# Separate PSUM tiles for the first feed-forward, W2 group 0 converted straight into SBUF, and eight float32 head pairs

## The chip, the cores and the metric

The kernel runs on one core of one Trainium2 chip. The metric is the device time of one execution in microseconds, lower is better. Engines are named as in the profile: PE is TensorE, DVE VectorE, ACT ScalarE, POOL GpSimd and SP the engine that issues the transfers.

## The reference

Three stages in a row: attention in which all scores lower than the row's maximum by more than tau are dropped, a feed-forward with SoLU and a layer norm, and a second, wider feed-forward with Mish.

```python
def _attn_ref(q, k, v, tau):                 # batch 4, heads 8, seq 576, head_dim 64
    scores = scale * np.matmul(q, k.transpose(0, 1, 3, 2))
    thresh = np.max(scores, axis=-1, keepdims=True) - tau
    scores = np.where(scores >= thresh, scores, -1000000000.0)
    scores = scores - np.max(scores, axis=-1, keepdims=True)
    attn = np.exp(scores)
    attn = attn / (np.sum(attn, axis=-1, keepdims=True) + 1e-09)
    return np.matmul(attn, v).astype(np.float32)

def _moe_ref(x, w_in, w_out, g_ln):          # 2304 tokens, 512 -> 1024 -> 512
    h = x @ w_in
    e = np.exp(h - np.max(h, axis=-1, keepdims=True))
    solu = h * (e / (np.sum(e, axis=-1, keepdims=True) + 1e-09))
    mu = np.mean(solu, axis=-1, keepdims=True)
    var = np.mean((solu - mu) ** 2, axis=-1, keepdims=True)
    ln = (solu - mu) / np.sqrt(var + 1e-06) * g_ln
    return (ln @ w_out).astype(np.float32)

def _moe2_ref(x, w_in, w_out):               # 512 -> 2048 -> 512
    h = x @ w_in
    sp = np.where(h > 20.0, h, np.log1p(np.exp(np.minimum(h, 20.0))))
    return ((h * np.tanh(sp)) @ w_out).astype(np.float32)
```

## The kernel before

**Numbers in two halves.** Most products are made from operands split into a high half in float32r and a low half (the difference), so that one float32 product becomes three float32r products (high by high, low by high, high by low). The four weight matrices come as float64 and are converted on the chip in blocks of 128 by 256: ACT makes a part from the low words (line 402) and clears the sign of the high words (line 408), DVE clamps and shifts (lines 410, 411) and joins the bits (line 413), POOL adds the two parts (line 415). `cr`, `cz`, `cl` and `cf` have two buffers each. Then ACT copies the high half and POOL subtracts for the low half.

**The order is planned.** Every step is a task with an engine, an estimated duration (`act`, `dve`, `gps`, `pe`, `dma`), what it waits for, and the buffers that it takes and uses. `Plan.run` tries several list schedules against these estimates and emits the instructions of each engine in the order of the shortest one. The engines then run in that order, and semaphores hold an instruction until its operands are there. Which instruction waits for which is worked out from the tiles that they read and write.

**Attention** goes over 16 pairs of heads; each pair has four blocks of 128 queries for each head and one block that the two heads share. `s_tile` makes scores on PE (line 505) in a PSUM buffer of two banks, DVE takes the maximum (line 511), ACT the exponential (line 513), DVE the threshold (line 516), POOL scales by the row's sum (line 530), PE transposes (lines 551, 554). For pairs from `F0` on, the transposed weights leave PSUM as a high half (ACT, line 538) and a low half (DVE, line 539), V is split too (lines 472, 473), and the products with V are two float32r products (line 588); the two halves of the result are added on POOL (line 605). Pairs before `F0` keep float32: one copy (line 536) and one float32 product (line 586).

**First feed-forward.** For each tile of 128 tokens `moe_h` makes h (line 642) in two halves of 512 columns, each taken out by ACT (line 650); `layer_norm` follows; `moe_t` transposes the result through the same PSUM buffer (line 692, taken out by lines 697 and 699); `moe_y` makes 256 tokens' y (line 713), taken out by ACT and DVE as high and low half (lines 723, 724) and stored. In PSUM all of this lies in one tile of two banks:

```python
    ms = pools(c1, PSUM)("p_ms").tile([128, 2, 512], F32, name="ms")
    smt = ms[:, 1, :PN]
    ...
    b_mo, b_s3 = Fixed(ms[:, 0]), Fixed(ms)
```

h and the transposes use the first bank (`b_mo`), y the second (`smt`), and in the first `M0` = 4 pairs a third of the score blocks uses both (`b_s3`).

**Second feed-forward.** W2 (both matrices of the second feed-forward) is used in four groups of 512 hidden features. `split_w2` brings a group into SBUF as AH, AL (first matrix) and BH, BL (second). Groups from `LATE` on are converted straight into these tiles: the conversion then clears the sign on DVE (line 405) and not on ACT, and the two halves are written by lines 825 (ACT) and 827 (POOL). Groups before `LATE`, here group 0, are converted ahead, stored to DRAM (line 428), loaded again (line 840) and split there (lines 847, 851). Group 0's tiles exist from `o_a` on, that is when the last scores and transposes of attention are done; those of group 1 from `o_c` on, when the first feed-forward is done. `ff_in` makes h (line 882), Mish and its two halves; `ff_out` makes o (line 908). The first `U0` = 6 pieces of group 0 are 256 tokens wide and run between the last tiles of the first feed-forward.

Of the kernel before, what the change touches and what calls it, by code (L numbers as in the profile page):

```python
# [8 lines left out]
F32 = mybir.dt.float32  # L9
# [3 lines left out]
ALU = mybir.AluOpType  # L13
# [9 lines left out]
class Task:  # L23
    def __init__(self, eng, dur, fn):
        self.eng, self.dur, self.fn = eng, dur, fn
# [13 lines left out]
class Buf:  # L39
# [4 lines left out]
    def new(self):  # L44
        self.slots.append(Slot(self, len(self.slots)))
        return self.slots[-1]


class Fixed(Buf):


    def __init__(self, part):
        super().__init__(None, None, None, None)
        self.part = part

    def new(self):
        x = super().new()
        x.take = lambda: setattr(x, "tile", self.part)
        return x


class Plan:
# [15 lines left out]
    def add(self, eng, dur, fn, deps=(), new=(), use=(), order=(), port=False, table=None):  # L78

        t = Task(eng, dur, fn)
        t.port, t.table = port or eng == "POOL", table
        t.new = list(new)
        t.need = [(d, True) for d in deps if d is not None] + [(d, False) for d in order if d is not None]
        for x in t.new:
            x.taker = t
            x.users.append(t)  # L90
        for x in use:
            x.users.append(t)
        self.tasks.append(t)
        return t
# [146 lines left out]
def kernel(  # L241
# [30 lines left out]
    PN = 256  # L272
    NG = 4
    FG = KF2 // NG
    NP = NT // PN
    F0 = 7
    M0 = 4
    LATE = 1
    U0 = 6

    def f(ap):
        return ap.bitcast(F32)

    def pools(stack, space=None, side=None):
        def pool(name, bufs=1):
            kw = {"space": space} if space is not None else {}
            if side is not None:
                kw["side"] = side
            return stack.enter_context(tc.tile_pool(name=name, bufs=bufs, **kw))
        return pool  # L290

    def act(n, psum=False):
        return (0.05 if psum else 0.094) + n / 1200

    def dve(n):
        return 0.069 + n * 1.042e-3
# [2 lines left out]
        return 0.069 + n * 0.52e-3  # L299

    def gps(n):
        return 0.149 + n * 2.1e-3

    def pe(count, n, passes=1):
        return count * (n / 2270 + 0.007 if passes == 1 else n * passes / 2400)
# [15 lines left out]
    def buf(p, tag, shape, dtype=F32, bufs=1):  # L321
        return Buf(lambda: P[p], tag, shape, dtype, bufs)
# [5 lines left out]
    wts = pool("wts")  # L328
    P["mo"] = pool("mo")
    P["small"] = small = pool("small")  # L330
    ms = pools(c1, PSUM)("p_ms").tile([128, 2, 512], F32, name="ms")
    smt = ms[:, 1, :PN]

    ident = const.tile([128, 128], F32, name="ident")
    tau_c = const.tile([128, 1], F32, name="tau_c")
# [118 lines left out]
    b_xo, b_tm = (buf("xs", n, [128, S], F32, c) for n, c in (("xo", 1), ("tm", 1)))  # L454
    b_st = buf("p_st", "st", [128, 2, 512], F32, 2)
    b_ta = buf("p_ta", "ta", [128, 512], F32, 2)
    b_mo, b_s3 = Fixed(ms[:, 0]), Fixed(ms)
    b_m = buf("small", "m", [128, 3], F32, 4)
    b_sr = buf("small", "sr", [128, 2], F32, 3)
    OPS, VL, E, EX, EVT, XST = ({} for _ in range(6))  # L460
    EXS, S3 = [], []

    def load_v(p):

# [11 lines left out]
    def operands(n):  # L476
        k2, q2, ks, qh, ql = (b.new() for b in (b_k2, b_q2, b_K, b_Q, b_L))
        lk, lq = (add("SP", dma(128 * w * 4), lambda slot=slot, src=src: D(slot.tile, src[n // H_, n % H_]), new=[slot])
                  for slot, src, w in ((k2, kk, S), (q2, qq, SP)))
        eng, e, cost = (V, "DVE", dve) if n < 2 else (G, "POOL", gps)  # L480
        a = add("ACT", act(S), lambda: SC.activation(ks.tile, k2.tile, ACTF.Copy), [lk], [ks], [k2])
        a2 = add(e, cost(S), lambda: eng.tensor_tensor(ks.tile[64:128], k2.tile[64:128], f(ks.tile[64:128]), ALU.subtract), [a], use=[ks, k2], port=True)  # L482
        b = add("ACT", act(SP), lambda: SC.activation(qh.tile, q2.tile, ACTF.Copy), [lq], [qh], [q2])  # L483
        b2 = add(e, cost(SP), lambda: eng.tensor_tensor(ql.tile, q2.tile, f(qh.tile), ALU.subtract), [b], [ql], [qh, q2], port=True)  # L484
        OPS[n] = [a, a2, b, b2], ks, qh, ql
# [36 lines left out]
    def weigh(p, i):  # L522

        e, sr, _, *ts = E[p, i]
        r = lambda h: sr.tile[:, h:h + 1]
        w = [add("DVE", 0.07, lambda h=h: V.tensor_scalar(r(h), r(h), 1.0e-9, None, ALU.add), [t], use=[sr]) for h, t in enumerate(ts)]
        t = add("DVE", 0.08, lambda: V.reciprocal(sr.tile[:, :len(ts)], sr.tile[:, :len(ts)]), w, use=[sr])  # L527
        for h in range(len(ts)):
            x = lambda h=h: e.tile[:, h * S:(h + 1) * S]
            E[p, i].append(add("POOL", 0.17 + S / 1000, lambda x=x, h=h: G.tensor_scalar(x(), x(), zero, r(h), ALU.add, ALU.mult), [t], use=[e, sr]))  # L530

    def leave(x, n, dst, src, dep, tp):

# [99 lines left out]
    def moe_h(t, j):  # L633
        if j == 0:
            x_split(t)
            SO[t] = [b_so.new()]
        so, (xh, xl) = SO[t][0], XSL[t]
        h, last_t = b_mo.new(), None

        def go(kt):  # L640
            for x, (l, r) in enumerate(((xh, W1H), (xh, W1L), (xl, W1H))):
                TE.matmul(h.tile, l.tile[:, kt], r[:, kt, j * 512:(j + 1) * 512],  # L642
                          start=(kt == 0 and x == 0), stop=(kt == KD - 1 and x == 2))

        for kt in range(KD):
            last_t = add("PE", pe(3, 512), lambda kt=kt: go(kt), XSP[t] + [W1T[kt, c] for c in range(j * 512, j * 512 + 512, CW)],
                         [h] if kt == 0 else (), [h, xh, xl], order=[last_t])
            if t == j == kt == 0:
                last_t.need += [(x, True) for x in S3[-1:]]
        SO[t].append(add("ACT", act(512, True), lambda: SC.activation(so.tile[:, j], h.tile, ACTF.Copy), [last_t],  # L650
                         [so] if j == 0 else (), [so, h], order=SO[t][1:]))
        if j:
            layer_norm(t)
# [50 lines left out]
    def moe_y(p, j):  # L704
        lh, ll = LN[p]
        c, half = divmod(j, 2)
        cs = slice(c * 128, (c + 1) * 128)
        y = smt
        ks = range(half * KF // 2, (half + 1) * KF // 2)

        def go(k):
            for x, (l, r) in enumerate(((W2H, lh), (W2L, lh), (W2H, ll))):
                TE.matmul(y, l[:, k, cs], r.tile[:, k], start=(k == 0 and x == 0), stop=(k == KF - 1 and x == 2))  # L713

        deps = TEV[p] + [W2T[k, c * 128 // CW * CW] for k in ks]
        t = Y0.get((p, c))
        for k in ks:
            t = add("PE", pe(3, PN), lambda k=k: go(k), deps + ([t] if t else Y0.get("last", [])), use=[lh, ll])
        Y0[p, c] = t
        if half == 0:  # L720
            return
        yh, yl = (b.new() for b in b_yy)
        a = add("ACT", act(PN, True), lambda: SC.activation(yh.tile, y, ACTF.Copy), [t], [yh])  # L723
        b = add("DVE", dve(PN), lambda: V.tensor_tensor(yl.tile, y, f(yh.tile), ALU.subtract), [a], [yl], [yh])  # L724
        Y0["last"] = [a, b]
        YST.setdefault(p, []).append(add("SP", dma(PN * 512), lambda: D(y_hi[p][cs, :], f(yh.tile)), [a], use=[yh]))
        YST[p].append(add("SP", dma(PN * 512), lambda: D(y_lo[p][cs, :], f(yl.tile)), [b], use=[yl]))


    for p in range(NH // 2 + 1):  # L730
        if p < NH // 2:
            operands(2 * p)
            operands(2 * p + 1)
            load_v(p)
        for i in range(QT):
            if p < NH // 2:
                for h in range(2 if i < KT else 1):
                    s_tile(p, i, h)
                weigh(p, i)
                for h in range(2 if i < KT else 1):  # L740
                    turn(p, i, h)
                turn(p, i, 2)
            if p and i == 0:
                pv(p - 1, 0, 1)
                pv(p - 1, 1, 1)
            if p < NH // 2 and i == 2:
                pv(p, 0, 0)
                pv(p, 1, 0)
    end_c3 = [t for ts in EXS for t in ts]
    pieces = []  # L750
    for t in range(NTILE + 1):
# [8 lines left out]

    W, W2Q = {}, {}

    def opens(fn, deps):

        return add("-", 0.0, fn, deps)

    def open_a():
        c3.close()
        P["w2a"] = pools(ctx, side="right")("w2a")
# [1 line left out]
    def open_b():  # L771
        c2.close()
        pool = pools(ctx, side="right")
        P["ffa"] = pool("ffa")
        P["hoa"] = pools(ctx, PSUM, "right")("hoa")

    def open_c():
        c1.close()
        pool = pools(ctx)
        P["w2b"] = pool("w2b")  # L780
        P["ffb"] = pool("ffb")
        P["hob"] = pools(ctx, PSUM)("hob")
        oa = pool("oa")
        acc.append(oa.tile([128, KD, NT], F32, name="acc"))

# [212 lines left out]
```

## Time and profile before

| what | before |
|---|---|
| median of three runs (range), us | 998.83 (997.68 to 999.58) |
| the profiled execution, us | 997.51 |
| its span, first to last instruction, us | 995.7 |
| PE busy, us (share of the span) | 934.4 (94%) |
| DVE busy, us | 639.2 (64%) |
| ACT busy, us | 594.8 (60%) |
| POOL busy, us | 422.8 (42%) |
| granted TensorE clock | 1.0 in every slice |

A row of the profile gives start and length of instructions, or sums over groups of them; times count from the start of the span. Idle time in front of an instruction is put down to what released it. Matmuls overlap one another, and their ends are modelled, so what PE loses in a wait is read from the starts.

### The profile page before, as it was taken

How to read it: one execution, taken by the hardware profiler on the slowest of the kernel's cores; microseconds unless marked ns; L12 is line 12 of the kernel's file. 1: busy time of each engine (PE TensorE's matmuls, PEld its weight loads, DVE VectorE, ACT ScalarE, POOL GpSimd, SP SyncE). 2: the span in 40 equal slices, each digit the busy share in tenths (PEclk: the TensorE clock that was granted, in tenths of full speed). 3: DMA queues.
4: the chain of work that ended last, by engine and by line, in shares of the span. 5: the costliest groups of instructions: out<-in, count | busy, mean ns of one | idle time of the engine just before them, and what ended most of it. 6: DMA issues, size and time to landing. Idle time of an engine off the chain costs nothing. (4 is left out here: it accounts for less than half of the span.)

```text
span 995.7 us, 16654 instructions
## 1 busy us (share of the span) xinstructions
PE 934.4 (94%) x5648; PEld 813.3 (82%) x5648; DVE 639.2 (64%) x1827; ACT 594.8 (60%) x1205; POOL 422.8 (42%) x446
## 2 busy tenths in 40 slices
PE   4899999989899999999889999999999999999998
PEld 4777777779788988888779888988888888888887
DVE  6898999998889989899865223135555445322222
ACT  5888988988778788786767364245433343222210
POOL 2878777877565566555451110123433133100000
PEclk9999999999999999999999999999999999999999
DMA  4444433324342223322474222397555245403312
GB/s 139 120 123 133 123 116 120 99 88 139 98 143 71 94 70 97 123 73 72 126 252 138 71 68 96 112 359 259 166 175 188 74 158 159 143 5 108 125 54 74
DMA packets 99942, 123.32 MB, mean 124 GB/s; under 512 B 9105, under 2 KB 72209, under 8 KB 99857
## 3 DMA queue, kind: packets, MB, share of 16 engines
q1 hardware_dynamic: 99712, 122.26, 38.9%
q8 instruction: 45, 0.74, 0.3%
q14 instruction: 41, 0.33, 0.1%
q10 hardware_dynamic: 144, 0.00, 0.0%
HBM read 98.11 MB, written 24.12 MB: 123 GB/s over the span
## 5 line engine op out<-in xcount | busy, mean ns | idle before, releaser
L530 POOL TENSOR_SCALAR e<-e,zero,sr 128x576 f32<-128x576 f32 x144 | 122.6, 859 | 66.6 <-DVE sr L527 46.1
L415 POOL TENSOR_TENSOR cf<-cf,cl 128x256 uint32<-128x256 uint32 x96 | 72.7, 765 | 153.9 <-DVE cf L413 116.4
L513 ACT ACTIVATE e<-st,m,sc 128x576 f32<-128x576 f32 x132 | 109.8, 835 | 31.0 <-DVE m L512 23.5
L516 DVE SCALAR_TENSOR_TENSOR e<-st,m,e 128x576 f32<-128x576 f32 x132 | 107.0, 813 | 12.8 <-ACT e L513 11.2
L505 PE MATMUL st<-Kst,Qhh 128*128 128x288 f32 (+2 forms) x312 | 94.4, 323 | 16.5 <-DVE Kst L482 10.4
L511 DVE TENSOR_REDUCE m<-st 128x1 f32<-128x576 f32 x132 | 98.7, 750 | 10.1 <-PE st L505 9.4
L713 PE MATMUL ms<-LH,W2H 128*128 128x256 f32 x288 | 86.1, 299 | 11.2 <-ACT so L650 7.8
L551 PE MATMUL ta<-ident,e 128*128 128x128 f32 x576 | 85.3, 277 | 8.2 <-ACT eyh L536 2.2
L505 PE MATMUL st<-Kst,Qb 128*128 128x288 f32 (+2 forms) x312 | 84.8, 296 | 0.0
L551 PEld LDWEIGHTS ta<-ident,e 128*128 128x128 f32 x576 | 66.8, 141 | 20.3 <-POOL e L530 7.3
L713 PE MATMUL ms<-LL,W2H 128*128 128x256 f32 x288 | 81.2, 282 | 0.0
L713 PE MATMUL ms<-LH,W2L 128*128 128x256 f32 x288 | 81.2, 282 | 0.0
L505 PEld LDWEIGHTS st<-Kst,Qhh 128*128 128x128 f32 x312 | 60.4, 194 | 23.4 <-DVE Kst L482 10.8
L642 PE MATMUL ms<-W1H,XH 128*128 128x512 f32 x144 | 62.0, 431 | 11.2 <-DVE yl L724 6.2
L932 DVE TENSOR_TENSOR acc<-acc,o 128x512 f32<-128x512 f32 x36 | 24.8, 688 | 70.8 <-PE o L908 70.6
L713 PEld LDWEIGHTS ms<-LH,W2H 128*128 128x128 f32 x288 | 54.5, 189 | 16.7 <-ACT so L650 11.3
L505 PEld LDWEIGHTS st<-Kst,Qb 128*128 128x128 f32 x312 | 60.5, 194 | 1.0
L484 POOL TENSOR_TENSOR Qb<-Q,Qhh 128x640 fp32r<-128x640 f32 x30 | 47.7, 1589 | 28.9 <-ACT Qhh L483 24.0
L402 ACT ACTIVATE cl<-cr 128x256 uint32<-128x256 uint32 x96 | 41.2, 438 | 30.1 <-DMA cr<-w_in 18.6
L642 PE MATMUL ms<-W1H,XL 128*128 128x512 f32 x144 | 56.7, 394 | 0.0
L642 PE MATMUL ms<-W1L,XH 128*128 128x512 f32 x144 | 56.6, 393 | 0.0
L887 ACT ACTIVATE n<-h 128x512 f32<-128x512 f32 x36 | 21.5, 597 | 58.3 <-PE h L882 58.2
(186 smaller groups left out, 2963.5 us busy)
## 6 DMA issues: line engine op xcount, KB each, us to landing
y5h<-y_hi SPq DMA_DIRECT2D x26, 512.0 KB, 5.9
y5l<-y_lo SPq DMA_DIRECT2D x26, 512.0 KB, 6.8
cr<-w_in SPq DMA_DIRECT2D x48, 256.0 KB, 3.2
cr<-w_out SPq DMA_DIRECT2D x48, 256.0 KB, 2.9
Q<-qq SPq DMA_DIRECT2D x32, 320.0 KB, 3.0
K<-kk SPq DMA_DIRECT2D x32, 288.0 KB, 2.9
y2h<-y_hi SPq DMA_DIRECT2D x10, 512.0 KB, 4.4
y2l<-y_lo SPq DMA_DIRECT2D x10, 512.0 KB, 5.4
```

The costliest lines, as they stand in the source:

```text
L402: t2 = add("ACT", act(CW), lambda: SC.activation(cl.tile, cr.tile[:, :, 0], ACTF.Copy, scale=2.0 ** -29), [t_f], [cl], [cr])
L415: t = add("POOL", gps(CW), lambda: G.tensor_tensor(cf.tile, cf.tile, cl.tile, ALU.add), [t4, t2], use=[cl, cf])
L484: b2 = add(e, cost(SP), lambda: eng.tensor_tensor(ql.tile, q2.tile, f(qh.tile), ALU.subtract), [b], [ql], [qh, q2], port=True)
L505: TE.matmul(st.tile[:, j, c - j * HS:c - j * HS + w], q.tile[:, i * 128:(i + 1) * 128], ks.tile[:, k0:k0 + w], start=(y == x == 0), stop=( ...
L511: t = add("DVE", dve(S), lambda: V.tensor_reduce(m.tile[:, 2:3], x(), AX.XY, ALU.max, negate=True), [t], [m], [st])
L513: a = add("ACT", act(S, True) + 0.18, lambda: SC.activation(et(), x(), ACTF.Exp, bias=m.tile[:, 0:1], scale=sc), [t], [e] if h == 0 else ( ...
L516: t = add("DVE", dve(S) + 0.06, lambda: V.scalar_tensor_tensor(et(), x(), m.tile[:, 1:2], et(), ALU.is_ge, ALU.mult, accum_out=sr.tile[:, ...
L530: E[p, i].append(add("POOL", 0.17 + S / 1000, lambda x=x, h=h: G.tensor_scalar(x(), x(), zero, r(h), ALU.add, ALU.mult), [t], use=[e, sr]))
L551: TE.transpose(tp.tile[:, k * 128:(k + 1) * 128], e.tile[:, o:o + 128], ident)
L642: TE.matmul(h.tile, l.tile[:, kt], r[:, kt, j * 512:(j + 1) * 512], start=(kt == 0 and x == 0), stop=(kt == KD - 1 and x == 2))
L713: TE.matmul(y, l[:, k, cs], r.tile[:, k], start=(k == 0 and x == 0), stop=(k == KF - 1 and x == 2))
L932: d = add("DVE", dve(512), lambda sums=sums, o=o: V.tensor_tensor(sums(), sums(), wide(o), ALU.add), pes + old, use=[o])
```

## The change

The tile `ms` goes. In its place the third score buffer `s3` (two banks) has a pool of its own, which is closed when the last score block that uses it is done (`o_s`); two pools of one bank each are then opened, `p_mo` for h and the transposes, `p_sm` for y. y's tile is taken anew for each block of 128 output rows, and the plan orders its use as it does for all other buffers, instead of by the entry `Y0["last"]`. The class `Fixed` is no longer needed. The PSUM pools of the second feed-forward change sides (left and right of PSUM).

`LATE` goes from 1 to 0: group 0 of W2 is converted straight into its tiles like the others; nothing is stored ahead.

`F0` goes from 7 to 8: pair 7 has float32 products with V too.

The planner's estimates for POOL change: `gps`, the low half of K (0.1 us more), and the scaling at line 530 (0.8 instead of 0.17 + 576/1000).

```diff
-class Fixed(Buf):
-
-
-    def __init__(self, part):
-        super().__init__(None, None, None, None)
-        self.part = part
-
-    def new(self):
-        x = super().new()
-        x.take = lambda: setattr(x, "tile", self.part)
-        return x
...
-    F0 = 7
+    F0 = 8
     M0 = 4
-    LATE = 1
+    LATE = 0
     U0 = 6
...
     def gps(n):
-        return 0.149 + n * 2.1e-3
+        return 0.16 + n * 2.15e-3
...
-    ms = pools(c1, PSUM)("p_ms").tile([128, 2, 512], F32, name="ms")
-    smt = ms[:, 1, :PN]
+    c0 = ctx.enter_context(ExitStack())
+    P["p_s3"] = pools(c0, PSUM, "right")("p_s3")
...
-    b_mo, b_s3 = Fixed(ms[:, 0]), Fixed(ms)
+    b_mo, b_s3 = buf("p_mo", "mo", [128, 512]), buf("p_s3", "s3", [128, 2, 512])
+    b_sm = buf("p_sm", "sm", [128, PN])
...
+    def open_s():
+        c0.close()
+        for n in ("p_mo", "p_sm"):
+            P[n] = pools(c1, PSUM, "right")(n)
...
-        a2 = add(e, cost(S), lambda: eng.tensor_tensor(ks.tile[64:128], k2.tile[64:128], f(ks.tile[64:128]), ALU.subtract), [a], use=[ks, k2], port=True)
+        a2 = add(e, cost(S) + (0.1 if e == "POOL" else 0.0), lambda: eng.tensor_tensor(ks.tile[64:128], k2.tile[64:128], f(ks.tile[64:128]), ALU.subtract), [a], use=[ks, k2], port=True)
...
-            E[p, i].append(add("POOL", 0.17 + S / 1000, lambda x=x, h=h: G.tensor_scalar(x(), x(), zero, r(h), ALU.add, ALU.mult), [t], use=[e, sr]))
+            E[p, i].append(add("POOL", 0.8, lambda x=x, h=h: G.tensor_scalar(x(), x(), zero, r(h), ALU.add, ALU.mult), [t], use=[e, sr]))
...
-                last_t.need += [(x, True) for x in S3[-1:]]
+                last_t.need.append((o_s, True))
...
-        y = smt
+        if half == 0:
+            Y0[p, c, "y"] = b_sm.new()
+        y = Y0[p, c, "y"]
...
-            t = add("PE", pe(3, PN), lambda k=k: go(k), deps + ([t] if t else Y0.get("last", [])), use=[lh, ll])
+            t = add("PE", pe(3, PN), lambda k=k: go(k), deps + ([t] if t else []), [] if t else [y], [lh, ll, y])
...
-        Y0["last"] = [a, b]
...
+    o_s = opens(open_s, S3)
...
-        P["hoa"] = pools(ctx, PSUM, "right")("hoa")
+        P["hoa"] = pools(ctx, PSUM)("hoa")
...
-        P["hob"] = pools(ctx, PSUM)("hob")
+        P["hob"] = pools(ctx, PSUM, "right")("hob")
```

## Rows read from the trace of the kernel before

**Rows 1.** Busy us (and instructions) of each engine in three stretches.

```profile
core 0: us, PE busy (x) PEld busy (x) DVE busy (x) ACT busy (x) POOL busy (x), PEclk, DMA share, GB/s
250.00:490.00 240.00, 223.75 (x1555) 201.55 (x1555) 218.19 (x668) 189.53 (x386) 139.83 (x128) 1.00 0.30 91
490.00:650.00 160.00, 148.81 (x1097) 139.38 (x1097) 62.31 (x143) 84.10 (x165) 31.31 (x33) 1.00 0.42 134
650.00:996.00 346.00, 341.85 (x1697) 288.01 (x1696) 132.81 (x292) 110.55 (x220) 66.91 (x88) 1.00 0.44 144
```

**Rows 2.** PE's waits from 250 to 490 us: waiter, releaser; us, times, longest.

```profile
PE ms L642 <- DVE yl L724: 3.4, 5, 1.4
...
PE ms L713 <- ACT so L650: 3.0, 6, 0.7
...
PE ms L642 <- ACT yh L723: 2.5, 4, 1.5
```

**Rows 3.** PE's waits from 490 to 650 us.

```profile
PE ms L713 <- ACT so L650: 3.5, 5, 0.7
PE ms L642 <- DVE yl L724: 2.9, 3, 1.0
PE ms L713 <- DVE yl L724: 2.3, 2, 1.2
```

**Rows 4.** PE in order of time near 558 us: start, length, idle before, releaser.

```profile
557.37 0.40 PE L642 MATMUL ms<-W1L,XH 128*128 128x512 f32 x1
557.60 0.39 PE L642 MATMUL ms<-W1H,XL 128*128 128x512 f32 x1
558.97 0.50 PE L642 MATMUL ms<-W1H,XH 128*128 128x512 f32 x1 [0.98 <-DVE yl L724]
```

**Rows 5.** The chain that ended last: start us, length, what.

```profile
510.40 0.61 ACT so L650
...
511.67 1.48 PE h L882 x12
...
530.58 1.43 PE o L908 x12
```

**Rows 6.** PE in order of time, float32 products, then split products.

```profile
192.72 2.32 PE L586 MATMUL ta<-eyh,V 128*128 128x320 f32 x8
194.88 0.70 PE L586 MATMUL ta<-evh,V 128*128 128x320 f32 x2
...
492.27 0.31 PE L588 MATMUL ta<-eyh,V 128*128 128x320 f32 x1
...
493.60 0.31 PE L588 MATMUL ta<-eyl,V 128*128 128x320 f32 x1
```

**Rows 7.** Groups by line: busy us, mean ns | idle before.

```profile
L415 POOL TENSOR_TENSOR cf<-cf,cl 128x256 uint32<-128x256 uint32 x96 | 72.7, 765 | 153.9 <-DVE cf L413 116.4 <-ACT cl L402 19.3 <-issue 9.2
...
L413 DVE SCALAR_TENSOR_TENSOR cf<-cr,cz 128x256 uint32<-128x256 uint32 x96 | 45.8, 492 | 4.3 <-POOL AL L827 1.2 <-issue 0.5 <-DMA w2o<-cf 0.4
...
L410 DVE TENSOR_SCALAR cz<-cz 128x256 f32<-128x256 f32 x96 | 33.3, 359 | 1.8 <-ACT cz L408 1.1
...
L539 DVE TENSOR_TENSOR eyl<-ta,eyh 128x512 fp32r<-128x512 f32 x45 | 30.3, 684 | 1.5 <-ACT eyh L538 1.3
```

**Rows 8.** POOL in order of time, low halves of W2 group 1.

```profile
641.54 1.44 POOL L827 TENSOR_TENSOR AL<-cf,AH 128x256 fp32r<-128x256 f32 x2 [26.64 <-ACT AH L825]
...
676.09 0.74 POOL L827 TENSOR_TENSOR AL<-cf,AH 128x256 fp32r<-128x256 f32 x1 [0.53 <-ACT AH L825]
```

**Rows 9.** Instructions of W2 group 0's store and load: ns min/median/max, first and last start.

```profile
L428 SPq DMA_DIRECT2D w2i<-cf x8: 320/338/447, 267.5 to 467.6; - x8
...
L840 SPq DMA_DIRECT2D AL<-w2i x4: 395/428/891, 491.1 to 492.5; - x4
```

**Rows 10.** POOL and DVE in order of time near 509 us.

```profile
508.08 1.23 POOL L673 TENSOR_SCALAR so<-so,nmu,rs 128x1024 f32<-128x1024 f32 x1 [0.69 <-DVE rs L672]
...
508.56 0.91 DVE L410 TENSOR_SCALAR cz<-cz 128x256 f32<-128x256 f32 x1 [0.32 <-ACT cz L408]
```

More of the change, by code (lines that the diff above doesn't have):

```diff
@@ L461, with opens @@
     EXS, S3 = [], []
+    def opens(fn, deps):
+        return add("-", 0.0, fn, deps)
+    def open_s():
+        c0.close()
+        for n in ("p_mo", "p_sm"):
+            P[n] = pools(c1, PSUM, "right")(n)
     def load_v(p):
@@ L712, in go @@
             for x, (l, r) in enumerate(((W2H, lh), (W2L, lh), (W2H, ll))):
-                TE.matmul(y, l[:, k, cs], r.tile[:, k], start=(k == 0 and x == 0), stop=(k == KF - 1 and x == 2))
+                TE.matmul(y.tile, l[:, k, cs], r.tile[:, k], start=(k == 0 and x == 0), stop=(k == KF - 1 and x == 2))
         deps = TEV[p] + [W2T[k, c * 128 // CW * CW] for k in ks]
@@ L722, in moe_y @@
         yh, yl = (b.new() for b in b_yy)
-        a = add("ACT", act(PN, True), lambda: SC.activation(yh.tile, y, ACTF.Copy), [t], [yh])
-        b = add("DVE", dve(PN), lambda: V.tensor_tensor(yl.tile, y, f(yh.tile), ALU.subtract), [a], [yl], [yh])
-        Y0["last"] = [a, b]
+        a = add("ACT", act(PN, True), lambda: SC.activation(yh.tile, y.tile, ACTF.Copy), [t], [yh], [y])
+        b = add("DVE", dve(PN), lambda: V.tensor_tensor(yl.tile, y.tile, f(yh.tile), ALU.subtract), [a], [yl], [yh, y])
         YST.setdefault(p, []).append(add("SP", dma(PN * 512), lambda: D(y_hi[p][cs, :], f(yh.tile)), [a], use=[yh]))
@@ L761 @@
     W, W2Q = {}, {}
-    def opens(fn, deps):
-        return add("-", 0.0, fn, deps)
     def open_a():
```

## Prediction

> **What bounds the kernel now.** I read the stretches first, then PE's waits in them, then single waits in order of time, then the chain that ended last. In the stretches [rows 1] the reader is to see two regimes. From 650 us to the end PE is busy 341.85 of the 345.7 us that are left of the span, so nothing there can shorten the time except less PE work. From 250 to 650 us PE is busy 93% and still sets the time: whatever it does not do there it does later, since all its work has to be done once. In 250 to 490 us DVE is nearly as full (218.19 of 240), ACT is at 79%, POOL at 58%; in 490 to 650 us DVE is at 39%. So a PE stall removed after 490 us should come back whole, and one removed before 490 us only as far as DVE lets the attention run faster.
>
> PE's waits say which stalls these are. Line 642 (the first feed-forward's h products) and line 713 (its y products) use different banks of one tile, `ms`. Yet h waits for the readers of y (lines 723, 724), and y waits for the reader of h (line 650) [rows 2, 3]. The code asks for none of these waits: the plan links h with h and y with y only. In time it looks so [rows 4]: h has issued its first three products at 557.60 us, then stops until yl of the *other* bank has been taken out, at 558.97. From one such product to the next it is ordinarily 0.23 us (557.37 to 557.60), here it is 1.37, so 1.14 us are lost where the view reports 0.98 idle; I add the difference, 0.16 us, to every wait of this kind. The chain that ended last [rows 5] runs through such a wait: ACT's eviction at line 650, 0.61 us at 510.40, is itself a link of it.
>
> **The change, part by part, against the profiled execution's 997.51 us.**
>
> *Separate tiles, after 490 us.* Rows 3 hold 3.5 + 2.9 = 6.4 us in 8 waits on the other bank; with 0.16 us each, 7.7 us. The third row there (y waiting for its own bank's yl, 2.3 us) is a true wait and stays. PE is the bound and DVE has room, so I take all of it: −7.7. Bounds: −7.7, and −4 if half come back as waits on the own bank, which has one buffer as before.
>
> *Separate tiles, 250 to 490 us.* Rows 2 hold 3.4 + 3.0 + 2.5 = 8.9 us in 15 waits, with 0.16 each 11.3 us. Here DVE is 91% busy: if PE's 240 us became 228.7, the same DVE work would fill 95% of them, so part is lost. Bounds 0 and −11.3; nearer to the latter, because PE is still the fuller of the two, and the next two edits take work from DVE. I take 70%: −8.
>
> *F0 = 8: pair 7 in float32.* Its attention-times-V products run as float32 (line 586) instead of high and low halves (line 588). Eight records with 320 columns take 192.72 to 194.88 us, 0.27 each; at line 588 nine take 492.27 to 493.60, 0.148 each [rows 6]. Either way a product is two records (in float32 one instruction that the trace shows as two, otherwise the high and the low half), and I scale one of 256 columns by its columns. A pair has 10 products of 320 and 10 of 256 columns: 20 × 0.27 × (1 + 0.8) = 9.7 us against 20 × 0.148 × 1.8 = 5.3, so PE gains 4.4 us of work. DVE loses the subtractions that make the low halves: by the code a pair has nine at line 539 with 512 columns (eight for its four query blocks and one for the shared block), 9 × 0.684 = 6.2 us [rows 7], and some small ones. Bounds: +4.4 (PE alone decides), −1.8 (DVE alone). PE is the one that is never free, so near the upper: +3.
>
> *LATE = 0: W2 group 0.* Removed: 16 stores of converted blocks and 8 loads back. Moved: 16 conversions, of which eight had been stored by 467.6 us [rows 9], now all finishing behind the gate `o_a`, since their ACT and POOL halves write straight into the W2 tiles. Only two converted blocks can stand ready before it (cf has two buffers). An early conversion costs DVE two TENSOR_SCALARs (lines 410 and 411, the same shape, 0.36 us) and line 413 at 0.49, 1.2 us together [rows 7]; a late one a third TENSOR_SCALAR in ACT's place, 1.6 in all. POOL has an addition of 0.77 for each and, where the low half is made, a second instruction of that shape. So before 468 us DVE is relieved of 8 × 1.2 = 9.7 us in a stretch where it is 91% full. Bounds 0 and −9.7; PE leads and the eight are spread over 200 us: −2.
>
> Behind the gate the question is whether the group comes late. The gate opens at about 491 us, where the old loads start [rows 9]. If DVE and POOL overlap fully, a conversion takes 1.6 us; if they exclude each other, 1.6 + 2 × 0.77 = 3.1. With two ready at 493, the eighth (all of the first matrix) is there at 493 + 6 × 3.1 = 512 at the slower of the two, and the twelfth (half of the second) at 524. Today the first h product of the second feed-forward starts at 511.67 and the first o product at 530.58 [rows 5]. So even at 3.1 us PE finds the weights nearly when it wants them; the last block, at 536, can hold up some o products. Bounds 0 and +6 (530.58 to 536); I take +1.5. Queued behind these on DVE, ACT and POOL are the layer norms of the last tiles, in a stretch where all three have room; SP issues 24 transfers fewer.
>
> That DVE and POOL can exclude each other is seen once [rows 10]: a 128x256 TENSOR_SCALAR on DVE takes 0.91 us instead of its mean of 0.36 and ends at 509.47, just behind the POOL instruction that ran from 508.08 to 509.31. The Trainium skill, "SBUF — State Buffer", section "Who interferes with whom", says that a DVE operation that uses both ports and a GpSimd operation lock each other out for a whole instruction, so it speaks against moving conversions to where they are wanted at once; by it this edit costs the 1.5 us, without it nothing.
>
> *Costs in the planner, pool sides.* No work; the order of instructions changes. Put at 0, ±3.
>
> Sum: −7.7 − 8 + 3 − 2 + 1.5 = −13.2, so 984.3 us in a profiled execution. The median of the runs shown (998.83) is 1.3 above the profiled one, which gives **985.6 us**.
>
> **Rivals.**
>
> *Larger gain.* The waits also block ACT and DVE, which stand in order behind the evictions, so their removal and the relief of DVE speed up the attention as well. Then nearly everything counts fully: −7.7 − 11.3 − 1.8 (the float32 pair by DVE) − 4.9 (half of the relief) = −25.7, with the 1.3 us to the median 973 us. For it: DVE at 91%. Against: PE at 93% in the same stretch; it cannot do both faster by more than its idle share of 16 us there.
>
> *Small gain.* Attention is held by DVE, so the stretch before 490 us gives nothing, the float32 pair costs its 4.4 and the own bank's single buffer takes half the later waits back: −4 + 4.4 − 2 to −7.7 + 3 − 2 + 1.5, that is about −2 to −5, 995 us. For it: the true wait in rows 3. At its weakest it is no change at all, which is also what follows if the waits are not due to the shared tile; against that speak the two lines in rows 4, which touch different banks.
>
> *Slower.* W2 group 0 comes late. In group 1 the eight conversions of the first matrix, which go the same way, had their low halves from 641.54 to 676.09 us [rows 8], 34.6 / 7 = 4.9 us apart. At that pace the twelfth block is ready at 493 + 10 × 4.9 = 542 and the last at 561, so o products stand 11 to 30 us behind where they stood, with some h products and the last layer norms as cover. At about 18 us this turns the sum into +4: 1003 us. It decides where the pace is above some 4.5 us. Against it: group 1 was not in a hurry at that time (its first use is far off), and POOL waited for DVE.
>
> **Chances.** A measurement of this kernel tells about 0.2% (2 us) from no change. Forecast (−8 to −19): 0.52. Larger gain: 0.18. Small gain of over 2 us: 0.13. Within 2 us: 0.05. Slower: 0.12. So faster 0.83, same 0.05, slower 0.12. The range reaches from the larger gain at 970 to no change at 1000; the likeliest case alone is 980 to 991.
>
> **What would show it.** In the profile after: no waits of line 642 on 723 or 724, nor of 713 on 650; waits of y on its own yl remain. Line 586 has 40 matmul records more and line 588 40 fewer. The gate `o_a` opens 5 to 8 us before 491 us. The first h product of the second feed-forward comes 15 to 21 us behind it, with no gap of PE over 1 us between. From about 637 us PE is full to the end. The forecast is wrong if PE shows new idle time between the gate and the first o product (slower), or if DVE, not PE, ends most waits of 250 to 480 us (small gain).

## Result and the profile after

The change takes 981.99 us in the median (980.56 to 983.27) against 998.25 us before, a ratio of 0.9835 (95% interval 0.9816 to 0.9854): 16.3 us faster, where 985.6 us, 12.7 less than the 998.3, had been forecast. The profiled execution took 983.27 us, its span is 981.5 us.

The stretches of the changed kernel, to be read against [rows 1]:

```profile
core 0: us, PE busy (x) PEld busy (x) DVE busy (x) ACT busy (x) POOL busy (x), PEclk, DMA share, GB/s
250.00:490.00 240.00, 227.01 (x1588) 207.31 (x1587) 217.31 (x651) 188.45 (x382) 134.44 (x124) 0.99 0.26 77
490.00:650.00 160.00, 155.40 (x1125) 146.77 (x1123) 73.50 (x175) 87.02 (x168) 46.35 (x50) 0.99 0.50 160
650.00:996.00 346.00, 327.19 (x1621) 275.54 (x1619) 129.20 (x279) 101.62 (x204) 64.51 (x84) 1.00 0.39 129
```

The last row is the shortest way to read the gain: PE is still full to the end, but only 327.19 us of work are left at 650 us, where it had been 341.85. PE was idle 4.6 us in 490 to 650 us (before 11.2) and 13.0 us in 250 to 490 (before 16.3).

PE's waits in the changed kernel, first from 250 to 490 us (the two longest), then all from 490 to 650 us:

```profile
PE ta L551 <- DVE exl L536: 2.5, 3, 1.1
PE st L502 <- DVE e L513: 2.1, 5, 0.7
...
PE sm L712 <- DVE yl L723: 2.7, 2, 2.4
PE sm L712 <- DVE nmu L662: 0.9, 1, 0.9
PE mo L689 <- ACT so L647: 0.8, 1, 0.8
```

The waits of [rows 2] and the first two of [rows 3] are gone: no h product waits for a reader of y, and no y product for the reader of h. What waits now waits for its own bank, or in attention. One is longer than any in rows 3: y waits once 2.4 us for its own yl.

That wait begins 8 us behind the last transposes of attention, the last of which now starts at 482.6 us (490.6 before, by the same view). The chain that ended last runs through it:

```profile
485.68 0.76 DVE cf L400
...
486.47 2.78 DMA cr<-w_in
...
489.27 0.15 ACT cl L389
489.42 2.67 DMA cr<-w_in
...
492.12 0.04 DVE cz L392
492.16 0.56 issue
492.72 0.42 DVE yl L723
...
493.19 4.54 PE sm L712 x24
...
498.66 3.12 PE sm L712 x24
```

Read from the top: DVE finishes a conversion (line 400) and so frees one of the two `cr` buffers; a block of W2 group 0 is loaded into it (2.78 us); ACT reads it, another block is loaded; DVE's clearing of the sign (line 392) waits for that block, and yl stands behind line 392 in DVE's queue; y on PE waits for yl. The 24 products that follow take 4.54 us, the next 24, which also follow a wait, 3.12.

POOL's low halves of W2 group 0 in the changed kernel, first and last of the first matrix, first and last of the second:

```profile
483.88 0.72 POOL L822 TENSOR_TENSOR AL<-cf,AH 128x256 fp32r<-128x256 f32 x1 [0.64 <-ACT AH L820]
...
506.78 0.73 POOL L822 TENSOR_TENSOR AL<-cf,AH 128x256 fp32r<-128x256 f32 x1 [0.53 <-ACT AH L820]
...
513.09 0.74 POOL L822 TENSOR_TENSOR BL<-cf,BH 128x256 fp32r<-128x256 f32 x1
...
538.32 1.22 POOL L822 TENSOR_TENSOR BL<-cf,BH 128x256 fp32r<-128x256 f32 x1 [0.53 <-ACT BH L820]
```

Eight blocks in 22.9 us and eight in 25.2, so 3.3 and 3.6 us apart.

### The profile page after: what moved, and what is told of

The parts are those of the page before. It is cut to its first block, busy times and chain, and to the rows that moved or that the text cites. A ratio compares the mean times of both kernels' runs of the same rounds, so it can differ in the third digit from the quotient of the medians.

```text
span 981.5 us, 16559 instructions
## 1 busy us (share of the span) xinstructions
PE 932.2 (95%) x5648; PEld 818.6 (83%) x5648; DVE 643.3 (66%) x1820; ACT 586.0 (60%) x1184; POOL 431.0 (44%) x452
## 4 chain that ended last, share of the span: by engine, by line
PE 72%; DVE 11%; ACT 8%; DMA 4%; issue 3%; POOL 1%; SPq 0%; DVEq 0%; POOLq 0%; ACTq 0%
PE o L903 14%; PE h L877 12%; PE ta L583 7%; PE sm L712 7%; PE h2b L877 7%; PE o2b L903 6%; PE mo L639 6%; PE st L502 5%; PE ta L548 3%; DVE m L508 3%; PE ta L585 3%; DVE e L513 2%; ACT e L510 2%; DMA cr<-w_in 2%; DMA cr<-w_out 1%
## 5 line engine op out<-in xcount | busy, mean ns | idle before, releaser
L402 POOL TENSOR_TENSOR cf<-cf,cl 128x256 uint32<-128x256 uint32 x96 | 74.8, 784 | 139.8 <-DVE cf L400 119.7
L712 PE MATMUL sm<-LH,W2H 128*128 128x256 f32 x288 | 84.9, 295 | 3.7 <-DVE yl L723 2.7
L712 PE MATMUL sm<-LL,W2H 128*128 128x256 f32 x288 | 81.9, 284 | 0.0
L712 PE MATMUL sm<-LH,W2L 128*128 128x256 f32 x288 | 81.8, 284 | 0.0
L639 PE MATMUL mo<-W1H,XH 128*128 128x512 f32 x144 | 62.1, 431 | 1.4 <-DVE LL L696 0.7
L712 PEld LDWEIGHTS sm<-LH,W2H 128*128 128x128 f32 x288 | 55.3, 192 | 5.8 <-DVE yl L723 3.8
L639 PE MATMUL mo<-W1H,XL 128*128 128x512 f32 x144 | 56.7, 394 | 0.0
L639 PE MATMUL mo<-W1L,XH 128*128 128x512 f32 x144 | 56.5, 392 | 0.0
```

What stands on the lines that cost most here:

```text
L402: t = add("POOL", gps(CW), lambda: G.tensor_tensor(cf.tile, cf.tile, cl.tile, ALU.add), [t4, t2], use=[cl, cf])
L712: TE.matmul(y.tile, l[:, k, cs], r.tile[:, k], start=(k == 0 and x == 0), stop=(k == KF - 1 and x == 2))
```

## Experiments

The theory was that the shared tile makes the waits and that their removal makes the gain, while the other edits cost a little. Its rival was that the gain comes from the other edits and the new order. Every kernel was compared with the kernel before on the same chip, so ratios are what is compared; 0.001 of a ratio is 1 us.

**The tiles alone, order kept.** The third score buffer's pool is closed, and the tiles of h and y are opened, when the first h tile is taken; the plan is not told of it, so that each engine issues the same sequence as before. In the two traces the instructions of every engine do stand in the same order.

```diff
+    def mo_pool():
+        if "p_mo" not in P:
+            c0.close()
+            P["p_mo"] = pools(c1, PSUM, "right")("p_mo")
+            smt.append(pools(c1, PSUM, "right")("p_sm").tile([128, PN], F32, name="sm"))
+        return P["p_mo"]
-    b_mo, b_s3 = Fixed(ms[:, 0]), Fixed(ms)
+    b_mo, b_s3 = Buf(mo_pool, "mo", [128, 512], F32), buf("p_s3", "s3", [128, 2, 512])
```

> The kernel before with nothing changed but the PSUM: h and y have a tile each, and every engine issues the same instructions in the same order as before. If the waits on the other bank were what the gain is made of (my theory, 7.7 us after 490 us and 70% of 11.3 us ahead of it): 998.3 - 15.7 = 982.5 us. If attention is held by DVE and gives nothing back: 998.3 - 7.7 = 990.5 us. If the gain came from the new order and the other edits: 996 to 998 us.

Measured: 974.96 us, ratio 0.9773 (0.9760 to 0.9787), that is 22.7 us less, more than any of the three expectations, and by the ratios some 6 us better than the full change. Its stretches, and all that PE waits for from 490 to 650 us; the last line is from PE's order of time:

```profile
250.00:490.00 240.00, 228.50 (x1612) 208.65 (x1611) 224.17 (x686) 197.47 (x413) 143.86 (x134) 1.00 0.34 103
490.00:650.00 160.00, 158.90 (x1158) 150.54 (x1157) 62.40 (x141) 81.67 (x153) 30.75 (x33) 1.00 0.51 166
650.00:996.00 346.00, 318.86 (x1567) 267.98 (x1565) 125.44 (x274) 101.31 (x202) 61.57 (x82) 1.00 0.37 121
...
PE sm L721 <- DVE yl L732: 1.1, 1, 1.1
...
488.19 0.39 PE L721 MATMUL sm<-LH,W2H 128*128 128x256 f32 x1 [1.85 <-DVE yl L732]
```

From 490 to 650 us PE is idle 1.1 us, and DVE got fuller in the stretch before (224.17 us instead of 218.19). The last of the transposes starts at 478.2 us, 12.4 earlier than before; the rest of the gain, some 10.6 us, lies behind them. A long wait of y for its own yl is here too, 1.85 us at 488.19, just ahead of the second stretch, although only five of the 16 blocks of W2 group 0 are still stored behind the last transposes (482.8 to 499.6 us).

**The changed kernel with one tile, order kept.** Here too the traces have the instructions of every engine in the same order.

```diff
+    ms = pools(c1, PSUM, "right")("p_ms").tile([128, 2, 512], F32, name="ms")
-    b_mo, b_s3 = buf("p_mo", "mo", [128, 512]), buf("p_s3", "s3", [128, 2, 512])
-    b_sm = buf("p_sm", "sm", [128, PN])
+    b_mo, b_s3 = Fixed(ms[:, 0]), Fixed(ms)
+    b_sm = Fixed(ms[:, 1, :PN])
```

> The changed kernel with h, y and the third score buffer back in one tile of two banks, every engine in the order of the changed kernel. Theory of the shared tile: the waits on the other bank come back, 982.0 + 16 = 998 us (up to 1003, as the new order was made without knowing of these waits, like the old one). Rival, that the other edits and the order made the gain: 982 to 986 us.

Measured: 997.28 us, ratio 0.9996 (0.9987 to 1.0006): nothing of the gain is left. PE's waits from 490 to 650 us show the pattern of rows 3 again:

```profile
PE ms L722 <- ACT so L657: 3.5, 5, 0.7
PE ms L649 <- DVE yl L733: 2.8, 3, 1.0
```

The two runs settle the main question from both sides. They also say that the other three edits together, with the new order, cost about 6 us beside separate tiles (0.9773 against 0.9835), and nothing that can be measured beside the shared one.

**Each of the other edits, in all combinations.** Six more kernels, each with separate tiles and one to three lines different (`LATE`, `F0`, the three estimates for POOL).

> The changed kernel with LATE = 1: W2 group 0 is converted ahead, stored and loaded again. My terms for this edit were -2 and +1.5, so undoing it gives 982.0 + 0.5 = 982.5 us, within the 3 us of a new order. If the conversions behind the gate hold PE up, which shows 2.6 us of new idle time at 493 us in the changed kernel: about 979 us. If the relief of DVE in the attention was worth more: 985 us or above.

> The changed kernel with F0 = 7: pair 7 again in high and low halves. My term was +3, so undoing it gives 982.0 - 3 = 979 us. If DVE decides in that stretch, its 6 to 8 us of subtractions come back against 4.4 us less on PE: 984 us.

> Separate tiles with before's order (975.0 us) and only the planner's new costs for POOL added: no work changes, only the order. My term was 0 within 3 us: 972 to 978 us. Rival, that the new costs give a worse order, which would explain why the changed kernel with F0 = 7 needs 989.4 us: 980 us or above.

> Separate tiles with the old costs and only F0 = 8 added: 4.4 us more work on PE, 7 us less on DVE. My term: +3, so 978 us. If DVE decides: 972 us or below. The planner makes a new order too, worth some us either way.

> Separate tiles with the old costs and only LATE = 0 added. My terms -2 and +1.5: 974.5 us. From the step between the changed kernel and the same with LATE = 1 (982.0 against 980.0): 977 us. If conversions behind the gate hold PE up: 980 us or above, with the first h product of the second feed-forward more than 25 us behind the last transposes of attention.

> The changed kernel with the planner's old costs for POOL: tiles, F0 = 8 and LATE = 0. If the new costs are what takes 7 us from the 975.0 of the tiles alone: about 975 us. If F0 = 8 and LATE = 0 take them: about 982 us as with the new costs.

With the tiles alone and the full change they make the whole cube:

| F0 | estimates | LATE 1: us, ratio | LATE 0: us, ratio |
|---|---|---|---|
| 7 | old | 974.96, 0.9773 (tiles alone) | 983.74, 0.9860 |
| 7 | new | 992.12, 0.9935 | 989.40, 0.9913 |
| 8 | old | 983.30, 0.9849 | 980.98, 0.9832 |
| 8 | new | 979.96, 0.9820 | 981.99, 0.9835 (full change) |

The intervals are 0.0013 to 0.0019 to either side. Two ways of writing the tiles are mixed in it: the first three of column LATE 1 and the first of LATE 0 have them as in the tiles alone, where the plan is not told of them, the other four as in the change. So only pairs of one kind are compared here. No edit has a price of its own. `LATE` = 0 costs 8.7 us in the first row and 1.5 in the last, where the intervals overlap. `F0` = 8 costs 7.6 us with the old estimates and LATE = 1, and gains 7.8 with the new ones and LATE = 0. The new estimates, which change no work at all, cost 16.2 us with F0 = 7 and LATE = 1, and 0.3, nothing that can be measured, with F0 = 8 and LATE = 0. Four of the six came out 5 to 17 us slower than my terms said. For the new estimates alone this can only be the order, and there the rival, a worse order, had number and cause right. For the others I put it down to the order as well, which is not shown for each. For `LATE` = 0 alone the rival, conversions that hold PE up, had the number, but its sign did not come: the first h product is 22.9 us behind the last transposes, not over 25. The change with `LATE` = 1 and the change with the old estimates came near what their rivals said (979 and 982), but within the noise of my own terms or of the full change, so they decide nothing.

Where the largest part of the 16 us of pure order goes is seen in the stretch 130 to 250 us, the row with the old estimates first, then with the new ones:

```profile
130.00:250.00 120.00, 113.53 (x699) 95.48 (x700) 113.98 (x358) 105.29 (x223) 93.44 (x95) 1.00 0.37 111
```

```profile
130.00:250.00 120.00, 106.41 (x626) 89.75 (x625) 111.74 (x345) 101.18 (x211) 88.20 (x90) 0.96 0.34 102
```

PE is busy 7.1 us less there and does 626 instead of 699 matmul records; the rest is spread over the other stretches. In order of time the second kernel's PE has one wait in attention that is far longer than its others (1.6 us at most from 20 us on):

```profile
195.47 0.70 PE L594 MATMUL ta<-evh,V 128*128 128x320 f32 x2
199.97 0.40 PE L513 MATMUL st<-Kst,Qhh 128*128 128x288 f32 x1 [3.80 <-DVE e L524]
...
201.23 3.84 PE L594 MATMUL ta<-eyh,V 128*128 128x320 f32 x8
```

Its next score product waits 3.80 us for the last reader of the score buffer, with no first feed-forward work placed between. Why the planner made that order is open.

**How much an order is worth.** The tiles alone, and the estimate for POOL 1 ns longer (`return 0.150 + n * 2.1e-3`).

> Separate tiles with before's settings and the planner's estimate for POOL 1 ns longer for each instruction: no work changes and no estimate gets better or worse, only the order comes out otherwise. If the order the planner happens to find is worth several us: 978 to 990 us. If an order is worth less than 2 us: 973 to 977 us, and then the new costs (992.1 us) are worse for a reason of their own.

Measured: 977.76 us, ratio 0.9807 (0.9794 to 0.9821), 3.4 us slower than without the nanosecond, by an order alone. That is just under the 978 expected if orders matter and just over the 977 if they do not; the intervals of the two kernels do not overlap.

**The float32 pair without a new order.** The tiles alone, planned with `F0` = 7; for pair 7 the high half is left whole, the low halves are not made, and the products are float32.

```diff
-        x += [t, add("DVE", dve(n), lambda: V.tensor_tensor(dst(lo)
+        x += [t, add("DVE", dve(n), lambda: None if full else V.tensor_tensor(dst(lo)
...
-                    if p < F0:
+                    if p == F32P:
+                        TE.matmul(acc.tile[:, :w], f(v.tile[:, k, 0:2]).rearrange("p a d -> p (a d)"), f(r), start=(k == 0), stop=(k == KT))
+                    elif p < F0:
```

> Separate tiles in before's order (975.0 us), and pair 7 in float32 with that order kept: its low halves (DVE, POOL and the second ACT copy) are left out and its products with V are float32. This is the work of F0 = 8 without a new order. My term was +3: 978 us. Bounds: +4.4 if PE alone decides (979.4), -1.8 if DVE does (973). The 983.3 us of F0 = 8 with a new order would then be order for the rest.

Measured: 976.14 us, ratio 0.9790 (0.9777 to 0.9804). Against the tiles alone that is +1.7 us, with intervals that overlap; +3 is not excluded, and the 7.6 us of the cube are mostly order.

**More buffers for the transfers behind the gate.** The changed kernel in its own order; the `cr` blocks taken behind the gate come from a pool with four buffers.

```diff
+        P["cv2"] = pools(ctx, side="right")("cv2")
-        self.tile = b.pool().tile(b.shape, b.dtype, tag=b.tag, name=b.tag, bufs=b.bufs)
+        late = b.tag == "cr" and "cv2" in b.pools
+        self.tile = (b.pools["cv2"] if late else b.pool()).tile(b.shape, b.dtype, tag=b.tag, name=b.tag, bufs=4 if late else b.bufs)
```

> The changed kernel in its own order; transfers of float64 blocks taken behind the gate get four buffers in place of two. Theory: behind the gate ACT and DVE stand in their queues for such a transfer, yl comes late and y on PE waits for it (2.6 and 1.1 us) and then runs 3.4 us at half clock. Then these go: 982.0 - 4 = 978 us. Rival, that the conversions there are limited by DVE and POOL excluding each other: 981 to 983 us.

Measured: 978.79 us, ratio 0.9818 (0.9805 to 0.9831), against 0.9835 of the change: 1.7 us less by the ratios, with overlapping intervals, 3.2 by the medians; by the time alone neither expectation is ruled out. The trace is clearer. The wait for yl, in the changed kernel and with four buffers:

```profile
493.19 0.58 PE L712 MATMUL sm<-LH,W2H 128*128 128x256 f32 x1 [2.40 <-DVE yl L723]
493.57 0.41 PE L712 MATMUL sm<-LH,W2L 128*128 128x256 f32 x1
493.78 0.41 PE L712 MATMUL sm<-LL,W2H 128*128 128x256 f32 x1
```

```profile
491.81 0.39 PE L714 MATMUL sm<-LH,W2H 128*128 128x256 f32 x1 [1.36 <-DVE yl L725]
```

One us of the 2.4 goes, and with it the stretch in which the products came 0.21 us apart. The transfer explains this part of the wait; the rest stays. What else makes yl late is seen in order of time, first POOL and DVE in the changed kernel, then DVE with four buffers:

```profile
489.23 1.43 POOL L602 TENSOR_TENSOR xo<-xo,tm 128x576 f32<-128x576 f32 x1 [0.16 <-ACT tm L597]
...
489.27 1.55 DVE L392 TENSOR_SCALAR cz<-cr 128x256 uint32<-128x256 uint32 x1
...
492.12 0.68 DVE L392 TENSOR_SCALAR cz<-cr 128x256 uint32<-128x256 uint32 x1 [0.57 <-DMA cr<-w_in]
...
498.56 0.28 DVE L392 TENSOR_SCALAR cz<-cr 128x256 uint32<-128x256 uint32 x1
```

```profile
488.95 1.54 DVE L394 TENSOR_SCALAR cz<-cr 128x256 uint32<-128x256 uint32 x1
...
491.14 0.28 DVE L394 TENSOR_SCALAR cz<-cr 128x256 uint32<-128x256 uint32 x1
491.34 0.41 DVE L725 TENSOR_TENSOR yl<-sm,yh 128x256 fp32r<-128x256 f32 x1
```

Clearing the sign (line 392, with four buffers 394) takes 0.28 us by itself and 1.55 beside POOL's addition of 1.43 us, just behind which it ends (490.82 against 490.66 us). That is DVE and POOL excluding each other, as in [rows 10] and as the rival has it, and more buffers leave it as it is. With them DVE no longer waits for the block (0.57 us), and the instruction behind that wait takes 0.28 us instead of 0.68. Of the 1.36 us that stay, taking y out accounts for some 0.8 us, since y has one buffer: 0.38 us for yh on ACT (at 490.48) and 0.41 for yl.

> Separate tiles in before's order, W2 group 0 converted ahead, and the same four buffers behind the gate. Here PE has only one wait over 1 us behind the gate, so the same 975 us within 1.5 us; better than that only if the later groups' conversions held PE up, which PE's full stretch to the end speaks against.

Measured: 975.03 us, ratio 0.9779 (0.9765 to 0.9792), as with two buffers. So more buffers for the later groups' loads bring nothing where PE has hardly a wait behind the gate. This kernel and the tiles alone are the fastest of the study.

## Why the prediction was right, point by point

- **The mechanism** was right: rows 4 showed waits on a bank that the waiting instruction does not touch, and both runs with a kept order show that they come from the shared tile.
- **The size of the tile term** was too small. I had −7.7 and −8; with before's order the tiles bring −22.7 (21.3 to 24.0), 12.4 us ahead of the last transposes and some 10.6 behind. The step that failed is "part is lost", the 70% for the stretch in which DVE is 91% full: DVE went to 93% and PE got all of it back. Besides, I had counted only the waits in rows 2 and 3. PE's waits of the whole kernel before have more of the kind:

```profile
PE ms L713 <- ACT so L650: 7.8, 13, 0.7
...
PE ms L692 <- ACT yh L723: 1.5, 3, 1.1
...
PE ms L642 <- DVE t L670: 0.9, 1, 0.9
...
PE ms L713 <- DVE LL L699: 0.4, 1, 0.4
```

  Of the first line 6.5 us in 11 waits were counted. In the second the transposes wait for a reader of y; the third is put down to yl in order of time (591.25 us); in the fourth y waits for a reader of the transposes. That makes 4.1 us more in seven waits, 5.2 with 0.16 us each. As an estimate from these rows, all of them bring 7.7 + 11.3 + 5.2 = 24.2 us, against 22.7 measured, so PE's waits are enough to account for the gain. The rival of the larger gain, with the waits in full (19 us), was nearer than my 15.7. Its reason, that ACT and DVE too stand behind the other bank's products, is seen (ACT's line 650 waited 3.2 us for y products from 250 to 490 us, and does not in the tiles alone), but what it is worth is not measured alone. In the changed kernel's own order the tiles bring 16 us (0.9996 to 0.9835), nearly my sum.
- **F0 = 8**, +3: by work alone +1.7, not distinguishable from +3. Line 583 (586 before) has 40 records more and line 585 (588) 40 fewer, as said.
- **LATE = 0, behind the gate**: the pace of 3.3 and 3.6 us is near the 3.1 that I had for DVE and POOL excluding each other. That they do is seen in single rows (line 392, 1.55 us instead of 0.28); the pace has the transfers in it as well, since with four buffers the first eight blocks came 2.9 us apart (483.55 to 504.04 us). The Trainium skill, "SBUF — State Buffer", section "Who interferes with whom", says that of a DVE instruction that uses both ports and a GpSimd one the first to come keeps the other out for its whole length. The row of line 392 agrees. But the price was put in the wrong place. I asked when the weights are there, and expected the first h product 15 to 21 us behind the gate with no gap of PE over 1 us. It starts at 511.4, 28.8 us behind, and no product waits for weights; the gap is 2.4 us. What I had waved through with "all three have room" is what happened: DVE stood in its queue for a transfer and behind POOL, and yl of the first feed-forward, which PE needed, stood behind it. Not all of the gap belongs to this edit, though: the tiles alone, with most of group 0 converted ahead, have 1.85 us at the same place.
- **Order**, 0 ± 3: the weakest step. The same work in another order differs by 3.4 us for a changed nanosecond and by 16 us for the new estimates. The change landed near its forecast because an underrated gain (7 us) met underrated costs of the other edits and their order (some 6 against my 2.5); so far its nearness is luck.
- **The other points**: the gate opened 8 us earlier (5 to 8 said); PE is full from well before 637 us. The slower rival did not come in: there is no stall on the weights of group 0, and from the gate to the first o product PE was idle 5.0 us, as before (4.9); the row before first, then the row after:

```profile
490.60:530.40 39.80, 34.90 (x242) 31.82 (x241) 25.85 (x63) 28.03 (x65) 16.04 (x19) 1.00 0.77 246
```

```profile
482.65:526.40 43.75, 38.77 (x256) 35.49 (x255) 30.82 (x74) 28.27 (x63) 25.02 (x28) 0.96 0.57 182
```

  The sign that I had given for the small gain did show: DVE ended 9.5 of the 12.1 us of PE's waits from 250 to 480 us (7.4 of 14.4 before). The gain was not small even so, so the sign was badly chosen: it tells what PE still waits for, not what it got back.

What stays open is how the 6 us divide between the work of LATE = 0 and order: LATE was not moved without a new order, and the cube shows nothing consistent. The profiled executions of the change and of the tiles alone (spans of 981.5 and 972.7 us) say only where the difference lies: 4.4 us ahead of the last transposes, 4.4 behind.

## What to carry to other kernels

Two buffers that take turns should be two tiles: in one tile, accesses to disjoint banks waited for each other here although the plan had them apart, and 2.3% of the time lay in it. A wait whose releaser works on other data than the waiting instruction is the sign to look for. And where a planner orders the instructions, an edit is measured only with the order kept; otherwise its price is hidden under that of a new order, here 3 to 16 us.

## What the runs showed of the hardware

The granted clock of PE fell to half for single short stretches in several of these kernels, but in the profiled executions of the kernel before and of the tiles alone it fell only at the very end. In the changed kernel it did so behind the 2.40 us wait: the columns are as in rows 1, the clock is the third number from the end, 0.51, that is 1.2 GHz of 2.4.

```profile
489.00:492.90 3.90, 1.78 (x15) 1.57 (x14) 3.28 (x6) 2.93 (x7) 2.96 (x4) 1.00 0.51 175
492.90:496.30 3.40, 3.11 (x14) 3.12 (x15) 3.22 (x9) 0.42 (x1) 1.87 (x2) 0.51 0.48 130
```

The same stretch with four buffers, where the wait is 1.36 us, has the full clock and 21 records instead of 14:

```profile
492.90:496.30 3.40, 2.46 (x21) 2.26 (x20) 3.18 (x9) 1.63 (x4) 2.78 (x3) 1.00 0.69 209
```

In the changed kernel products of 256 columns come 0.21 us apart there (493.57 to 493.78) instead of 0.12, and the 24 behind the wait take 4.54 us where the next 24, behind a wait at the full clock, take 3.12: the half clock cost PE 1.4 us beyond the wait.

The length of one wait does not decide it. In the changed kernel the clock fell once more, among waits of 0.47, 1.00 and 0.46 us from 295 to 298.5 us. And one and the same wait can go either way: in the tiles alone the products behind the 1.85 us at 488.19 ran at the full clock (1.00 from 485 to 495 us), while the same kernel with four buffers, every engine in the same order, had half of it behind the same 1.85 us. The rows are of the changed kernel, then of the tiles alone with four buffers:

```profile
298.40:301.70 3.30, 3.23 (x12) 3.23 (x13) 3.30 (x15) 0.65 (x3) 0.00 (x0) 0.50 0.12 41
```

```profile
488.35 0.39 PE L723 MATMUL sm<-LH,W2H 128*128 128x256 f32 x1 [1.85 <-DVE yl L734]
...
488.90:492.10 3.20, 3.20 (x17) 3.20 (x17) 3.20 (x7) 1.74 (x6) 1.67 (x2) 0.50 0.73 195
```

The stretch 130 to 250 us with the new estimates, mean clock 0.96, has half the clock behind its 3.80 us wait: eight records that took 2.32 us in [rows 6] take 3.84. It has it a second time, from 225 to 231 us, behind waits of 1.27 and 1.15 us.

Executions of one kernel differ in the granted clock, and in time with it. Of the eleven of the changed kernel with one tile, the five with a granted clock of 1.000 took 996.26 to 997.18 us, the two with 0.998 took 998.29 and 998.80, the two with 0.996 took 999.59 and 999.88.
